# Pinning TensorE's order by unit, moving mask and output steps behind maxima, and one subtraction to GpSimd, in an attention and token-mixing kernel

## Chip, cores and metric

One core of a Trainium2 chip. The metric is the device time of one launch in microseconds (us). The engines are TensorE (PE in the profile; its weight loads are PEld), VectorE (DVE), ScalarE (ACT), GpSimd (POOL) and SyncE (SP), which issues DMAs.

## What is computed

Three stages, cut to what matters (B = 2, H = 8, S = 768, D = 64, 16 clusters, model width 512, all float32):

```python
def _attn_ref(q, k, v, centroids):
    q_n, k_n, c_n = (x / (norm(x) + 1e-6) for x in (q, k, centroids))
    q_assign = argmax(einsum('bhsd,hcd->bhsc', q_n, c_n), -1)
    k_assign = argmax(einsum('bhsd,hcd->bhsc', k_n, c_n), -1)
    mask = q_assign[:, :, :, None] == k_assign[:, :, None, :]
    scores = where(mask, scale * q @ k.transpose(0, 1, 3, 2), -1e9)
    attn = exp(scores - max(scores, -1))
    return attn / (sum(attn, -1) + 1e-9) @ v

def _moe_ref(x, w_tok1, w_tok2, w_ch1, w_ch2):
    u = x + (relu(x.transpose(0, 2, 1) @ w_tok1) @ w_tok2).transpose(0, 2, 1)
    return u + relu(u @ w_ch1) @ w_ch2

def _moe2_ref(x, w_theta, w_tok_r, w_tok_i, w_ch):
    theta = x @ w_theta
    u = x + w_tok_r @ (x * cos(theta)) + w_tok_i @ (x * sin(theta))
    return u + relu(u @ w_ch)
```

A query attends only to the keys of its own cluster. The attention's output is the x of the second stage, whose output is the x of the third.

## The kernel before

Attention runs over 48 units of 256 queries of one head (`units`, three per head, six per pair of heads). A loop over n issues three stages of three neighbouring units. `scores(n)` (L385) makes two tiles s in PSUM, each of 128 queries by 768 keys: each half of 384 keys is a product of the query with the key and its low part (L392 and L397; qh, k1) and a second one that carries the query's low part and the one-hot rows of the clusters (L398; q2, k2), with a large negative number where clusters differ. VectorE takes the maximum of a tile (nm, L400), ScalarE the exponential (e, L402). `turn(n-1)` (L411) transposes e of the unit before in 12 products into three tiles t of the pool ps_t (L417), which ScalarE (two) and VectorE (one) copy to p (L420, L422). `values(n-2)` (L426) multiplies p with v into o (L438), 12 products; its two halves are added by tmp on ScalarE (L445) and an addition on VectorE into xt (L447). PSUM holds two banks of s (ps_s), three of t (ps_t, which sim, pp and x use too) and one of o (ps_o).

Around these three stand other steps. `masks` (L238) is a generator, of which the loop takes two steps for each n: similarities of q and k with the centroids (sim, L246), their transposing on VectorE (sT, L252), maximum (mx, L256), equality (eq, L259) and transposing (eqT, L265), a product with a triangular matrix (pp, L270) that keeps the first maximum of equal ones, the one-hot rows (oh, L271) and m (L286); `place` copies the rows of m by DMA into q2 and k2 (L358). `natural` (L453) transposes xt of a finished pair of heads back into rows (x, six products in two banks of ps_t, L460) and VectorE multiplies them with the reciprocal sums into xn (L462). `split_pair` and `prep` load and split the next q and k (GpSimd, DMAs of SP). `load_w` (L100) loads and repairs weights: L109 and L110 on ScalarE, L112 and L113 on VectorE, L116, L80 and L86 on GpSimd or VectorE. For the first head the one-hot rows are written by engines and not by DMA (L276 and L280 on ScalarE, L279 on VectorE), and `prep_pair_first` (L309) splits the key by L314 and L316.

After attention come the token products (`tok_up` g, with gh on ScalarE at L147 and gl on VectorE at L148; `tok_down` h; `tok_x` splits x by xh, L84, and xl, L86), then the channel products and the third stage, all as triples of products of high and low parts (L126 to L128).

The order inside each engine is fixed when the program is built: a scheduler places the instructions by its own simulation, and `tc.issue_after(...)` ties a step behind a marked one. Each engine then runs its row in order, and waits at an instruction's head for what it needs.

## Time and profile before

| | |
|---|---|
| median of 3 runs | 665.26 us (663.36 to 665.73) |
| profiled execution | 664.99 us, span 663.3 us |
| TensorE busy | 646.8 us (98% of the span), 3591 products |
| TensorE weight loads | 517.7 us (78%) |
| VectorE busy | 401.2 us (60%) |
| ScalarE busy | 344.9 us (52%) |
| GpSimd busy | 257.6 us (39%) |

A row of the timeline gives the start in us, the duration, engine, line, operation, out<-in, tile size and how many stand in the row; in brackets the idle time of the engine before it and what released it. Ends of products on TensorE are modelled, so distances of starts are firmer than durations. The attention takes the first 240 us or so.

### The profile page before, as it was taken

To read this page: it belongs to the slowest core of one execution; us is meant where nothing else is said; L and a number is where in the kernel's file an instruction comes from. 1 tells how busy PE (TensorE), PEld (TensorE's weight loads), DVE (VectorE), ACT (ScalarE), POOL (GpSimd) and SP (SyncE) were. 2 spreads that over 40 slices of the span, in tenths; PEclk is the share of its full clock that TensorE was granted. 3 is DMA by queue.
4 is the path that set the end of the run, shared out by engine and by line. 5 is a ranking of instruction groups with operands and counts; after the bars stand their busy time and mean duration, and the time that the engine had idled before them with its cause. 6 is when DMAs were issued, how large, how long until landed. Compare 5 with 4: busy or idle time off the path is not lost.

```text
span 663.3 us, 9795 instructions
## 1 busy us (share of the span) xinstructions
PE 646.8 (98%) x3591; PEld 517.7 (78%) x3591; DVE 401.2 (60%) x649; ACT 344.9 (52%) x653; POOL 257.6 (39%) x231
## 2 busy tenths in 40 slices
PE   7999999999999989999999999999999999999998
PEld 4777777777777758878888888888887878888886
DVE  5877778687787776466665442546677694531212
ACT  5676776777767863256444320428487673320000
POOL 6230312364031131138887520603467796541000
PEclk9999999999999998999999999999999999999999
DMA  8554755444555121023433310310021424300001
GB/s 294 160 138 105 169 123 144 120 117 114 113 123 124 37 96 47 18 67 124 154 133 127 126 53 14 95 33 0 1 85 42 128 88 127 114 20 33 16 33 47
DMA packets 24207, 61.42 MB, mean 93 GB/s; under 512 B 4256, under 2 KB 7520, under 8 KB 24160
## 3 DMA queue, kind: packets, MB, share of 16 engines
q1 hardware_dynamic: 24160, 60.80, 32.3%
q8 instruction: 28, 0.46, 0.3%
q14 instruction: 19, 0.16, 0.1%
HBM read 39.65 MB, written 3.15 MB: 65 GB/s over the span
## 4 chain that ended last, share of the span: by engine, by line
PE 86%; ACT 4%; DVE 3%; POOL 3%; issue 2%; DMA 2%; SPq 0%; POOLq 0%; ACTq 0%
PE o L438 10%; PE t L417 9%; PE s L397 5%; PE r L126 5%; PE r L127 5%; PE r L128 5%; PE c L126 5%; PE c L127 5%; PE c L128 5%; PE s L398 5%; PE y L128 4%; PE y L127 4%; PE y L126 4%; PE po L126 2%; PE po L128 2%
## 5 line engine op out<-in xcount | busy, mean ns | idle before, releaser
L402 ACT ACTIVATE e<-s,nm 128x768 f32<-128x768 f32 x96 | 86.7, 905 | 29.4 <-DVE nm L400 28.1
L400 DVE TENSOR_REDUCE nm<-s 128x1 f32<-128x768 f32 x96 | 90.5, 951 | 18.9 <-PE s L398 18.0
L417 PE MATMUL t<-ident,e 128*128 128x128 f32 x576 | 80.5, 275 | 0.6 <-ACT p L420 0.5
L417 PEld LDWEIGHTS t<-ident,e 128*128 128x128 f32 x576 | 66.4, 140 | 16.0 <-issue 9.4
L397 PE MATMUL s<-k,qh 128*128 128x384 f32 x188 | 71.9, 382 | 2.5 <-ACT e L402 2.3
L438 PE MATMUL o<-p,vs 128*64 128x256 f32 x564 | 71.2, 388 | 0.0
L398 PE MATMUL s<-k,q 128*128 128x384 f32 x192 | 65.3, 343 | 2.4 <-DVE q L279 2.4
L420 ACT ACTIVATE p<-t 128x512 f32<-128x512 f32 x96 | 52.2, 594 | 25.4 <-PE t L417 25.0
L126 PE MATMUL r<-ul,c_h 128*128 128x512 f32 x144 | 56.5, 396 | 0.4 <-DVE ul L90 0.4
L126 PE MATMUL y<-zl,k_h 128*128 128x512 f32 x144 | 56.1, 390 | 0.0
L128 PE MATMUL y<-zh,k_h 128*128 128x512 f32 x144 | 56.1, 390 | 0.0
L127 PE MATMUL r<-uh,c_l 128*128 128x512 f32 x144 | 56.1, 390 | 0.0
L127 PE MATMUL y<-zh,k_l 128*128 128x512 f32 x144 | 56.0, 389 | 0.0
L127 PE MATMUL c<-c_h,rl 128*128 128x512 f32 x144 | 56.0, 390 | 0.0
L128 PE MATMUL r<-uh,c_h 128*128 128x512 f32 x144 | 56.0, 390 | 0.0
L128 PE MATMUL c<-c_h,rh 128*128 128x512 f32 x144 | 55.9, 390 | 0.0
L126 PE MATMUL c<-c_l,rh 128*128 128x512 f32 x144 | 55.2, 391 | 0.0
L438 PEld LDWEIGHTS o<-p,vs 128*64 128x64 f32 x564 | 36.3, 136 | 22.7 <-issue 5.9
L116 POOL TENSOR_TENSOR c_f<-c_f,c_raw 128x512 uint32<-128x512 uint32 x24 | 31.6, 1318 | 44.7 <-issue 31.3
L80 POOL TENSOR_SCALAR qh<-ql 128x768 fp32r<-128x768 f32 x7 | 5.8, 835 | 100.9 <-DMA qh<-qh 100.8
L397 PEld LDWEIGHTS s<-k,qh 128*128 128x128 f32 x188 | 35.4, 188 | 11.1 <-ACT e L402 5.6
L398 PEld LDWEIGHTS s<-k,q 128*128 128x128 f32 x192 | 36.7, 192 | 3.8 <-ACT k L276 3.4
(192 smaller groups left out, 1387.9 us busy)
## 6 DMA issues: line engine op xcount, KB each, us to landing
c_raw<-wc SPq DMA_DIRECT2D x24, 512.0 KB, 3.3
k_raw<-wri SPq DMA_DIRECT2D x18, 512.0 KB, 3.5
qh<-qh SPq DMA_DIRECT2D x28, 192.0 KB, 3.0
k<-kh SPq DMA_DIRECT2D x28, 192.0 KB, 3.8
ql<-qT SPq DMA_DIRECT2D x8, 384.0 KB, 3.2
kl<-kT SPq DMA_DIRECT2D x8, 384.0 KB, 4.6
vs<-v SPq DMA_DIRECT2D x16, 192.0 KB, 2.4
w_raw<-w SPq DMA_DIRECT2D x6, 512.0 KB, 4.1
```

Of the source, the lines that this page charges most:

```text
L80: nc.gpsimd.tensor_scalar(out=h, in0=x, scalar1=1.0, scalar2=0.0, op0=ALU.mult, op1=ALU.add)
L116: nc.gpsimd.tensor_tensor(out=wu, in0=wu, in1=lo, op=ALU.add)
L126: nc.tensor.matmul(ps, ah, bl, start=first and i == 0, stop=False)
L127: nc.tensor.matmul(ps, al, bh, start=False, stop=False)
L128: nc.tensor.matmul(ps, ah, bh, start=False, stop=last and i == n - 1)
L397: nc.tensor.matmul(ps[:, half, :NH], qh[:, c], k1[:, n], start=True, stop=False)
L398: marks["scores"] = nc.tensor.matmul(ps[:, half, :NH], ql[:, c], kk[:, n], start=False, stop=True)
L400: marks["max"] = nc.vector.tensor_reduce(out=nm, in_=ps[:, :, :NH], axis=AX.XY, op=ALU.max, negate=True)
L402: marks["exp"] = nc.scalar.activation(out=e.rearrange("p (a n) -> p a n", a=2), in_=ps[:, :, :NH], func=AF.Exp, bias=nm, accum_out=sums[b, ...
L417: marks["turn"] = nc.tensor.transpose(ps[:, a, i * P : i * P + P], es[i][:, kt * P : kt * P + P], ident)
L420: marks["pA"] = nc.scalar.activation(out=p, in_=ps, func=AF.Copy)
L438: nc.tensor.matmul(po[r : r + 64, :], vs[:, kt, :], pr[kt // 2][:, kt % 2, :], start=kt < 2, stop=kt >= NT - 2, tile_position=(0, r),)
```

## The change

It has four parts.

1. In `prep_pair_first` the subtraction that makes the first key's low part (64 x 768) is issued by GpSimd and no longer by VectorE; the mark "k1", behind which `clear(1)` is issued, is now that subtraction.
2. For the first unit's scores, all products and not only the second ones are issued behind the first one-hot product (pp).
3. `scores(n)` is issued behind the last product of `values` issued before it, and `turn(n-1)` behind the last product of `scores(n)` (for n > 2).
4. `natural` of a pair comes two steps of the loop later (n + 3 for n + 1) and behind the last maximum issued before; the masks' two steps of a loop step move from ahead of `turn` to the end of the loop step, behind a maximum as well.

```diff
@@ prep_pair_first
-            marks["k1"] = nc.gpsimd.tensor_scalar(out=k1[0:64, :], in0=k, **one)
+            nc.gpsimd.tensor_scalar(out=k1[0:64, :], in0=k, **one)
             nc.scalar.activation(out=qh[0:64, :], in_=q, func=AF.Copy, scale=scale)
-            nc.vector.tensor_tensor(out=k1[64:128, :], in0=k, in1=k1[0:64, :].bitcast(F32), op=ALU.subtract)
+            marks["k1"] = nc.gpsimd.tensor_tensor(out=k1[64:128, :], in0=k, in1=k1[0:64, :].bitcast(F32), op=ALU.subtract)
@@ scores
-                if first:
-
-                    for half in range(2):
-                        nc.tensor.matmul(ps[:, half, :NH], qh[:, c], k1[:, half * NH : half * NH + NH], start=True, stop=False)
                 with tc.issue_after(marks["cl"].ins) if first else nullcontext():
                     for half in range(2):
                         n = slice(half * NH, half * NH + NH)
-                        if not first:
-                            nc.tensor.matmul(ps[:, half, :NH], qh[:, c], k1[:, n], start=True, stop=False)
+                        nc.tensor.matmul(ps[:, half, :NH], qh[:, c], k1[:, n], start=True, stop=False)
@@ values
-                    nc.tensor.matmul(
+                    marks["o"] = nc.tensor.matmul(
@@ the loop over n
                 if n != 1:
-                    es[n] = scores(b, h, u, ops[b, h])
+                    with tc.issue_after(marks["o"].ins) if "o" in marks else nullcontext():
+                        es[n] = scores(b, h, u, ops[b, h])
...
-            if n >= 3:
-                for _ in range(PACE):
-                    next(gen, None)
...
-                prs[n - 1] = turn(*units[n - 1], es.pop(n - 1))
+                with tc.issue_after(marks["scores"].ins) if n > 2 else nullcontext():
+                    prs[n - 1] = turn(*units[n - 1], es.pop(n - 1))
...
-                    late.append((n + 1, b, h // 2))
+                    late.append((n + 3, b, h // 2))
             while late and (n >= late[0][0] or n == len(units) + SKEW - 1):
                 _, b, pr = late.pop(0)
-                natural(b, pr)
+                with tc.issue_after(marks["max"].ins):
+                    natural(b, pr)
+            if n >= 3:
+
+                with tc.issue_after(marks["max"].ins):
+                    for _ in range(PACE):
+                        next(gen, None)
```

Three places show what the scheduler makes of it. Lines of the changed kernel are lower by five from the scores on (L392 and L393 for L397 and L398, L412 for L417, L433 for L438, L440 for L445, L455 for L460).

First, TensorE at the start, behind the first similarities. Before:

```order
L392 MATMUL s_194<-k_169,qh_168 128x384 x2
L392 MATMUL s_203<-k_169,qh_168 128x384 x2
L270 LDWEIGHTS ltri
L270 MATMUL pp_183<-eqT_180,ltri 128x384
L398 MATMUL s_194<-k_0_151,q_0_149 128x384
L398 MATMUL s_203<-k_0_151,q_0_149 128x384
```

Changed:

```order
L270 LDWEIGHTS ltri
L270 MATMUL pp_183<-eqT_180,ltri 128x384
L392 MATMUL s_194<-k_169,qh_168 128x384
L392 MATMUL s_203<-k_169,qh_168 128x384
L393 MATMUL s_194<-k_0_151,q_0_149 128x384
L392 MATMUL s_194<-k_169,qh_168 128x384
L393 MATMUL s_203<-k_0_151,q_0_149 128x384
L392 MATMUL s_203<-k_169,qh_168 128x384
```

The one-hot product (pp) stands ahead of all products of the two first tiles, and the second halves of the products with qh stand among those with the one-hot rows.

Second, TensorE in a unit in the middle of attention (o: values, s: scores, t: transposes). Before:

```order
L438 MATMUL o_537<-p_472,vs_249 64x256 x2
L438 MATMUL o_537<-p_479,vs_249 64x256 x2
L438 MATMUL o_537<-p_486,vs_249 64x256 x2
L397 MATMUL s_549<-k_454,qh_453 128x384
L398 MATMUL s_549<-k_0_151,q_0_149 128x384
L397 MATMUL s_549<-k_454,qh_453 128x384
L398 MATMUL s_549<-k_0_151,q_0_149 128x384
L417 MATMUL t_594<-ident,e_505 128x128 x2
L417 MATMUL t_601<-ident,e_505 128x128 x2
L417 MATMUL t_608<-ident,e_505 128x128 x2
L397 MATMUL s_558<-k_454,qh_453 128x384
L398 MATMUL s_558<-k_0_151,q_0_149 128x384
```

Changed:

```order
L433 MATMUL o_537<-p_472,vs_249 64x256 x2
L433 MATMUL o_537<-p_479,vs_249 64x256 x2
L433 MATMUL o_537<-p_486,vs_249 64x256 x2
L392 MATMUL s_549<-k_454,qh_453 128x384
L393 MATMUL s_549<-k_0_151,q_0_149 128x384
L392 MATMUL s_549<-k_454,qh_453 128x384
L393 MATMUL s_549<-k_0_151,q_0_149 128x384
L392 MATMUL s_558<-k_454,qh_453 128x384
L393 MATMUL s_558<-k_0_151,q_0_149 128x384
L392 MATMUL s_558<-k_454,qh_453 128x384
L393 MATMUL s_558<-k_0_151,q_0_149 128x384
L412 MATMUL t_594<-ident,e_505 128x128 x2
```

The unit's eight score products stand together, and all transposes behind them. In the order of before, 21 output groups are followed by transposes and 18 by scores; now one and 32.

Third, ScalarE at the end of attention (gh: the token product's split; w_2, c_0: weights; xh: splits of x). Before:

```order
L445 ACTIVATE tmp_3247<-olast 64x256
L147 ACTIVATE gh_3286<-g_3267 128x512
L109 ACTIVATE w_2_f<-w_2_raw 128x512
L84 ACTIVATE xh_3312<-xn_72 128x512
L84 ACTIVATE xh_3316<-xn_73 128x512
L147 ACTIVATE gh_3308<-g_3267 128x512
L84 ACTIVATE xh_3320<-xn_74 128x512
```

Changed:

```order
L440 ACTIVATE tmp_3247<-olast 64x256
L109 ACTIVATE w_2_f<-w_2_raw 128x512
L147 ACTIVATE gh_3286<-g_3267 128x512
L84 ACTIVATE xh_3312<-xn_72 128x512
L84 ACTIVATE xh_3316<-xn_73 128x512
L84 ACTIVATE xh_3320<-xn_74 128x512
L84 ACTIVATE xh_3324<-xn_75 128x512
L84 ACTIVATE xh_3328<-xn_76 128x512
L84 ACTIVATE xh_3332<-xn_77 128x512
L109 ACTIVATE c_0_f<-c_0_raw 128x512
L110 ACTIVATE c_0_raw<-c_0_raw 128x512
L147 ACTIVATE gh_3308<-g_3267 128x512
```

The second gh stands behind four more xh and behind two steps of the load of c_0. From the last transposes of attention on, TensorE's own order is the same in both.

## Rows read from the trace of the kernel before

**Rows 1.** Busy time by stretch: us, PE, PEld, DVE, ACT, POOL, PEclk, DMA share, GB/s

```profile
20.00:242.00 222.00, 218.99 (x1619) 167.04 (x1619) 171.15 (x300) 162.27 (x343) 57.41 (x50) 1.00 0.49 118
```

**Rows 2.** Timeline of TensorE, units in the steady stretch

```profile
62.90 1.52 PE L438 MATMUL o<-p,vs 128*64 128x256 f32 x12
...
67.20 1.51 PE L438 MATMUL o<-p,vs 128*64 128x256 f32 x12
...
83.12 0.47 PE L397 MATMUL s<-k,qh 128*128 128x384 f32 x1
...
84.65 1.47 PE L417 MATMUL t<-ident,e 128*128 128x128 f32 x12
86.05 1.52 PE L438 MATMUL o<-p,vs 128*64 128x256 f32 x12
87.50 0.66 PE L417 MATMUL t<-ident,e 128*128 128x128 f32 x4
```

**Rows 3.** List of TensorE's waits: total us, times, longest

```profile
PE s L397 <- ACT e L402: 2.3, 4, 0.6
```

**Rows 4.** Timeline of TensorE, one such wait

```profile
55.40 0.34 PE L398 MATMUL s<-k,q 128*128 128x384 f32 x1
56.36 0.44 PE L397 MATMUL s<-k,qh 128*128 128x384 f32 x1 [0.62 <-ACT e L402]
56.64 0.34 PE L398 MATMUL s<-k,q 128*128 128x384 f32 x1
```

**Rows 5.** Timeline of all engines, the start

```profile
6.90 0.49 PE L246 MATMUL sim<-kl,cst 128*32 128x384 f32 x2
7.65 0.95 DVE L316 TENSOR_TENSOR k<-kl,k 64x768 fp32r<-64x768 f32 x1 [0.72 <-POOL k L314]
9.84 0.56 DVE L259 TENSOR_TENSOR eq<-sT,mx 128x384 bf16<-128x384 f32 x1
11.63 1.80 POOL L306 TENSOR_TENSOR k<-kr,k 64x768 fp32r<-64x768 f32 x1
12.02 1.63 DVE L279 CAST q<-oh 16x384 fp32r<-16x384 f32 x1
12.07 1.06 ACT L276 ACTIVATE k<-oh 16x384 fp32r<-16x384 f32 x2 [1.36 <-DVE oh L271]
13.79 1.62 PE L398 MATMUL s<-k,q 128*128 128x384 f32 x4 [2.41 <-DVE q L279]
16.12 0.90 ACT L402 ACTIVATE e<-s,nm 128x768 f32<-128x768 f32 x1 [0.42 <-DVE nm L400]
```

**Rows 6.** Timeline of VectorE, the end of a pair

```profile
55.47 1.26 DVE L462 TENSOR_TENSOR xn<-x,ri 128x128 f32<-128x128 f32 x6
```

**Rows 7.** The page's costliest groups, then the timeline round a weight load

```profile
L400 DVE TENSOR_REDUCE nm<-s 128x1 f32<-128x768 f32 x96 | 90.5, 951 | 18.9 <-PE s L398 18.0
...
207.59 0.67 ACT L109 ACTIVATE w_f<-w_raw 128x512 f32<-128x512 f32 x1
208.15 0.70 ACT L110 ACTIVATE w_raw<-w_raw 128x512 uint32<-128x512 uint32 x1
210.33 0.42 DVE L447 TENSOR_TENSOR xt<-o,tmp 64x256 f32<-64x256 f32 x1
211.15 1.52 PE L438 MATMUL o<-p,vs 128*64 128x256 f32 x12
```

**Rows 8.** Timeline after attention

```profile
250.34 0.63 ACT L84 ACTIVATE xh<-xn 128x512 fp32r<-128x512 f32 x1 [0.65 <-PE g L126]
254.53 0.60 ACT L147 ACTIVATE gh<-g 128x512 fp32r<-128x512 f32 x1 [3.57 <-PE g L128]
255.03 2.19 ACT L84 ACTIVATE xh<-xn 128x512 fp32r<-128x512 f32 x4
255.16 0.69 DVE L148 SCALAR_TENSOR_TENSOR gl<-g,gh 128x512 fp32r<-128x512 f32 x1 [1.46 <-ACT gh L147]
256.38 0.39 PE L126 MATMUL h<-gl,w_h 128*128 128x512 f32 x1
```

## Prediction

> **What bounds the kernel now.** I read the busy time by stretch first. Between 20 and 242 us, the steady part of attention, TensorE is busy for 218.99 of 222.00 us, while VectorE, ScalarE and GpSimd are busy for 171.15, 162.27 and 57.41 us, at a granted clock of 1.00 [rows 1]. So the end is set by TensorE's row of instructions, and a change of order can do two things only: alter what a step costs TensorE (a switch from one kind of product to another), or take away and bring in waits. All that TensorE idles here is 3.0 us, 1.4% of the stretch.
>
> The timeline of TensorE gives the price of a unit [rows 2]. From one output group to the next, with transposes and scores interleaved, it is 67.20 - 62.90 = 4.30 us. Ungrouped pieces stand there too: eight scores 84.65 - 83.12 = 1.53, twelve transposes 86.05 - 84.65 = 1.40, an output group 87.50 - 86.05 = 1.45.
>
> The list of waits says what TensorE stood for: 2.3 us, four times, before scores for an exponential [rows 3]. The timeline shows one of them [rows 4]: the next unit's first score comes at 56.36 instead of right behind 55.40, since its bank holds scores whose exponential is late. Starts show more than the profile's idle does, because ends are modelled. The score products of a row follow each other by 0.17 (eight in 1.53, the first with a switch); here the distance is 56.36 - 55.40 = 0.96, and the one after it 56.64 - 56.36 = 0.28. So 0.79 + 0.11 = 0.90 is lost where 0.62 is counted: 1.45 for each us counted.
>
> **The change, part by part**, against the profiled execution (664.99 us, span 663.3), which is 0.27 below the median of 665.26.
>
> *Start.* The subtraction of the first key's low part (L316, 0.95 us) goes from VectorE to GpSimd. Behind it on VectorE stand the transposing of the similarities, their maximum and eq. TensorE's sim products end at 6.90 + 0.49 = 7.39 [rows 5], so these steps could run 1.2 us earlier, and eq at 8.64 instead of 9.84. But GpSimd's own subtraction of 64x768 takes 1.80 us (L306, of the same shape) and would run from 7.65 to 9.45, across eq. What such company costs is seen with the copy of the one-hot rows: 16x384 elements take 1.63 us, from 12.02 to 13.65, ending 0.22 after L306 does at 13.43 [rows 5]. So I let eq end at 9.9 instead of 10.40: 0.5 gained, and eqT, the product pp and oh behind it come 0.5 sooner. Before, TensorE's second products stood until 13.79, for the copy of 1.63 us; that copy now runs ahead of L306 instead of beside it, and the last to come are ScalarE's rows of the key, which ended at 12.07 + 1.06 = 13.13 and now end at 12.6. So this wait ends 1.1 sooner. But the second halves of the first products now stand behind pp and among the second products: two more are done before the first maximum can start. At the 1.62 / 4 = 0.4 that these take, 0.8 of the 1.1 is lost; at the 0.17 of a later score 0.3 is. The first exponential (16.12) so starts 0.3 to 0.8 sooner; I take the value nearer to the later one, **-0.7**. If eq is not held at all, 0.7 more is gained (-1.4); if the copy falls beside two GpSimd operations in a row, the start loses up to 0.5.
> The Trainium skill, "SBUF — State Buffer", section "SBUF: two separate sides", says that VectorE and GpSimd hold a shared port pair as an exclusive lock for a whole instruction, also for a VectorE operation with two SBUF inputs against one of GpSimd that reads SBUF. By that, eq would start only at 9.45 and end at 10.0, and the start would gain 0.6 instead of 0.7. The copy of 1.63 us beside GpSimd bears the rule out.
>
> *Order in a unit.* Scores now follow the last output product, and transposes follow the scores. By [rows 2] the grouped unit costs 1.53 + 1.40 + 1.45 = 4.38, against 4.30. In the order of before 20 units went from outputs to transposes and now go to scores; the others had the new sequence already. 20 x 0.08 = 1.6; the 1.53 has a product of the masks beside it, so I take **+1.5**, between 0 and 1.6. Grouping gains nothing: no piece is shorter in it.
>
> *Old waits.* The natural steps stood on VectorE ahead of a maximum (six multiplies, 1.26 us, from 55.47 [rows 6], just before the exponential was late); they now stand behind it. So do the masks' steps: each moves by a maximum (0.95 [rows 7]) at most, with the copies of m's rows that SP issues after them; those keep their place in SP's order and have several units until their head comes, so I cost the move at nothing. If they were late, their head's scores would wait up to 1 us for each pair. All of the 3.0 us goes, by starts 3.0 x 1.45: **-4.3** (-3.0 by the profile's idle).
>
> *New waits.* (a) The six multiplies of a pair now stand behind a maximum. The first group of x transposes (four) fills one of three banks of ps_t, the second (two) another, with scores of the next unit between; then that unit's transposes want the bank back. VectorE's chain is four multiplies (4 x 0.21), an addition of the output (L447, 0.42), a maximum (0.95 on average) and two multiplies (0.42) [rows 6, 7], 2.6 in all and 2.8 with the steps from engine to engine; TensorE has eight scores (1.53), two transposes of x (2 x 0.117) and two banks of unit transposes (8 x 0.117) [rows 2] in the same time, 2.7. That is 0.1 late, and 0.2 with the bank's own step; I take 0.2 for each of six pairs: +1.2; none if the maximum comes first, 1.15 if a second one comes between. (b) The single output bank is freed by tmp on ScalarE and the addition on VectorE. In two units weight loads (L109 0.67, L110 0.70) now stand ahead of tmp. The slack is seen at 210.33: the addition ends at 210.75 and the next outputs start at 211.15, 0.40 later [rows 7]. 1.37 - 0.40 = 0.97, of which I take 0.9 twice: +1.8. (c) The last pair's unit transposes wait behind four multiplies: +0.8. Together **+3.8**, between 0 and 9.5 (six times 0.95 more).
>
> *After attention.* The order of ScalarE puts the second gh behind four more xh and two steps of the load of c_0. In the profile of before, gh starts when TensorE's last g product is done (254.53), four xh take 2.19 from 255.03, gl ends at 255.85 and h, which reads it, starts at 256.38: 0.53 of slack [rows 8]. The xh wait for TensorE to finish with buffers (250.34, 0.65 idle), so not all of them can run ahead. At least c_0's two steps (0.67 + 0.70) delay gh: 1.37 - 0.53 = **+0.8**; at most all six, 2.19 + 1.37 - 0.53 = 3.0; nothing if buffers come free in time.
>
> Sum: -0.7 + 1.5 - 4.3 + 3.8 + 0.8 = +1.1, so 666.1 for the profiled execution and, 0.27 higher, **666.4 us** as a median. From the last transposes on TensorE's order is the same to the end, so nothing is added there.
>
> **Rivals.** 0.5% is 3.3 us, about what a measurement of this kernel can tell from no change.
>
> *A, the old waits go and nothing takes their place.* For it: VectorE has 51 us free in the stretch [rows 1], and 2.8 against 2.7 in (a) is close to even. Against: three banks and one output bank as before, and a weight load ahead of tmp. -0.7 + 1.5 - 4.3 = -3.5, so 661.5, as a median 661.8 us; without the 1.5 of order 660.3. It decides where VectorE gets x's second group multiplied before the unit's maximum. Chance 0.16.
>
> *B, slower: natural waits a whole maximum more.* The multiplies may begin only when a maximum is done, and maxima come in twos. If x's second group stands behind both, each pair costs 0.95 more: 6 x 0.95 = 5.7, so 671.8, as a median 672.1 us. It decides when VectorE is late by more than 0.5 us, half a maximum, at the pair's end. For it: the pairs' ends are where before was late, too [rows 4]. Against: the first unit behind a pair has 0.95 x 2 + 0.85 of work for VectorE in 4.3 us. Chance 0.10; 0.02 more for the ends of several bounds at once.
>
> *C, TensorE has room that the busy time hides.* Weight loads are busy only 167.04 of 222.00 us [rows 1]. If grouping let products run at the pace of their loads, up to 55 us would go: 610 us. Against: the grouped pieces cost 4.38 where interleaved ones cost 4.30 [rows 2]. Chance 0.01.
> The Trainium skill, "Perfetto Trace Analysis", section "Identifying the Most-Contended Engine", holds that matmul busy time is no good measure of what is left on TensorE, and that the busy share of weight loads is; here that would be 75%, and the pieces' rows do not bear out that order could win it.
>
> *Nothing moves* (the pinned order repeats what the scheduler had) is a case of the forecast: 665.3 us.
>
> **How the numbers follow.** The forecast, between 662 and 668.5, has 0.71. The lower end has to reach A, 661.0; the upper end takes in half of what B adds (2.9) and stops at 669.3; B and the rest beyond leave under 0.2 out. Faster: A and C, 0.17. Slower: 0.12.
>
> **What would show it.** In the new profile: the first exponential at 15.4, within 0.5, and GpSimd's subtraction at 7.65, 1.8 long. The waits of scores for exponentials, 2.3 us before, gone from the list. The unit of one output group to the next at 4.36 to 4.38. In their place short waits, on x or t for VectorE's multiplies at the pairs' ends, on o at two units with a weight load, and about 0.8 us at the first h. The busy time of TensorE in the stretch should stay within 2 us of 219. The prediction is wrong if the waits of TensorE in attention sum to under 1.5 or over 8 us, or if the grouped unit is under 4.25.

## The result, and the profile after

The changed kernel took 670.74 us (670.67 to 670.79, 3 runs) against 665.26: a ratio of 1.0084, interval 1.0063 to 1.0105. The forecast was no change, at 666.4 in a range up to 669.3; the changed kernel came out slower, and above that range. Run again in six more executions beside 20 of the kernel before, it took 667.19 against 663.81, 1.0052 [1.0033, 1.0071]: it is slower, by some 3.4 us. The profiled one of the first three executions held a further loss that will be found below; the other two left no trace, so that they had the same loss is likely by their times, but not shown.

The profiled execution of the changed kernel took 670.74 us, span 669.0. Lines from the scores on are lower by five than before (L392 and L393 scores, L412 t, L433 o, L457 xn; L643 and L644 make rh and rl in both). Page, busy time and instructions by engine:

```profile
PE 648.8 (97%) x3591; PEld 520.5 (78%) x3591; DVE 403.3 (60%) x648; ACT 341.7 (51%) x653; POOL 260.2 (39%) x232
```

TensorE does the same 3591 products in 648.8 us of work, 2 us more than before; the rest of the 5.7 us of span is idle. Busy time of the steady stretch, to lay beside [rows 1] (same columns):

```profile
20.00:242.00 222.00, 218.47 (x1615) 168.34 (x1609) 169.46 (x297) 158.05 (x339) 57.57 (x50) 1.00 0.48 118
```

The stretch looks the same: 3.5 us idle instead of 3.0. So most of the time was not lost in attention. The list of TensorE's waits over the whole execution (us in total, times, longest) says where idle time went:

```profile
PE g L126 <- DVE gl L148: 3.8, 1, 3.8
PE o L433 <- DVE xt L442: 2.1, 3, 1.2
...
PE c L126 <- ACT rh L643: 1.3, 1, 1.3
...
PE t L412 <- DVE xn L457: 1.0, 4, 0.5
...
PE c L127 <- DVE rl L644: 0.8, 1, 0.8
PE h L126 <- DVE gl L148: 0.6, 1, 0.6
```

The waits of scores for exponentials [rows 3] are gone; one of 0.3 stands at the start, ahead of that stretch. Waits of o on the output addition and of t on x's multiplies stand in their place, as foreseen. Three groups stand after attention: g on gl (2.6 us before), h on gl, which the prediction had, and c on rh and rl, which no part of it had. None of the signs that the prediction named for being wrong came: from 20 to 242 us the waits of TensorE come to 3.1 us, and an ordinary unit takes 4.34 to 4.42. What broke the forecast lies behind attention.

A better way to place the loss than busy time is to lay the starts of the same products beside each other. Where the distance grows, time is lost:

| start of | before | changed | difference |
|---|---|---|---|
| first output product | 24.05 | 22.71 | -1.34 |
| last output product | 242.62 | 242.35 | -0.27 |
| first u (transposes after the token products) | 270.66 | 272.57 | +1.92 |
| c, 145th product (channel products, second round) | 382.91 | 384.82 | +1.92 |
| c, 169th product | 388.52 | 394.51 | +5.99 |
| last po product (end) | 659.82 | 665.56 | +5.74 |

So -1.34 at the start, +1.07 in attention, +2.19 in the 28 us after it, +4.07 within 24 channel products at 385 us, -0.25 behind. The loss of 4.07 us lies 140 us behind the last product of attention.

That loss in the timelines of TensorE and ScalarE of the changed kernel (start, us, engine, line, operation, idle before and releaser):

```profile
386.64 0.39 PE L128 MATMUL c<-c_h,rh 128*128 128x512 f32 x1
388.32 0.47 PE L126 MATMUL c<-c_l,rh 128*128 128x512 f32 x1 [1.29 <-ACT rh L643]
389.60 0.50 PE L127 MATMUL c<-c_h,rl 128*128 128x512 f32 x1 [0.81 <-DVE rl L644]
...
390.80 0.63 PE L128 MATMUL c<-c_h,rh 128*128 128x512 f32 x1
```

```profile
382.42 0.60 ACT L643 ACTIVATE rh<-r 128x512 fp32r<-128x512 f32 x1
386.49 0.65 ACT L110 ACTIVATE th_raw<-th_raw 128x512 uint32<-128x512 uint32 x1 [3.47 <-DMA th_raw<-wth]
387.04 0.64 ACT L109 ACTIVATE th_f<-th_raw 128x512 f32<-128x512 f32 x1
387.59 1.07 ACT L643 ACTIVATE rh<-r 128x512 fp32r<-128x512 f32 x2
```

ScalarE stands 3.47 us for a load of w_theta that nobody needs yet; rh, which TensorE needs, is next but one in its row. TensorE waits 1.29 and 0.81 us, then works at half clock for a while (products of 0.63 for 0.39; the granted clock is 0.53 from 392 to 394, so nearly all of that at the lower of its two levels, 1.2 for 2.4 GHz). In the kernel before, the same load was ready at 382.10 and rh just in time. The load came late because the stream of weights, in which each load waits for a buffer of the third one ahead, had lost 2.1 us at one load of 512 KB. The DMA view of that load's stretch (queue, packets, MB, share; then the issue, KB and us from issue to landing), changed kernel, from 352.0 to 357.2:

```profile
q1 hardware_dynamic: 205, 0.71, 38.9%
q8 instruction: 1, 0.02, 1.1%
...
c_raw<-wc SPq DMA_DIRECT2D x1, 512.0 KB, 5.2
```

and of the same load in the kernel before, from 349.5 to 354.7:

```profile
q1 hardware_dynamic: 212, 0.74, 40.7%
...
c_raw<-wc SPq DMA_DIRECT2D x1, 512.0 KB, 3.1
```

In the first there is one packet of instructions, 16 KB that some 256 of TensorE's instructions take, and the load needs 5.2 us for 3.1. In the packets of the trace it runs from 354.44 to 355.32; eight packets of the load then run one behind the other from 355.30 to 357.1, when all its others were done at 355.3. The trace names no DMA engine for a packet: that these eight stand behind the instructions on one of the 16 is read from their times. In the kernel before the nearest such packet came at 355.37, 2.7 us behind the load's last.

So I had two theories. **F**: the loss at 386 us is a late load (by a meeting with a packet of instructions) that reaches TensorE because rh stands behind a step waiting for loads on ScalarE; what is left is the order of gl after attention. **R**: the loss is rival B's, multiplies behind maxima, and whatever is seen later follows from it.

### The profile page after: what moved, and what is told of

The parts are those of the page before. It is cut to its first block, busy times and chain, and to the rows that moved or that the text cites. A ratio compares the mean times of both kernels' runs of the same rounds, so it can differ in the third digit from the quotient of the medians.

```text
span 669.0 us, 9862 instructions
## 1 busy us (share of the span) xinstructions
PE 648.8 (97%) x3591; PEld 520.5 (78%) x3591; DVE 403.3 (60%) x648; ACT 341.7 (51%) x653; POOL 260.2 (39%) x232
## 5 line engine op out<-in xcount | busy, mean ns | idle before, releaser
L397 ACT ACTIVATE e<-s,nm 128x768 f32<-128x768 f32 x96 | 86.8, 904 | 21.7 <-DVE nm L395 21.5
L415 ACT ACTIVATE p<-t 128x512 f32<-128x512 f32 x96 | 54.9, 596 | 37.9 <-PE t L412 37.2
L412 PE MATMUL t<-ident,e 128*128 128x128 f32 x576 | 72.4, 273 | 1.4 <-DVE xn L457 1.0
L433 PE MATMUL o<-p,vs 128*64 128x256 f32 x564 | 71.2, 388 | 2.1 <-DVE xt L442 2.1
L392 PE MATMUL s<-k,qh 128*128 128x384 f32 x192 | 71.5, 373 | 0.4 <-ACT e L397 0.3
L412 PEld LDWEIGHTS t<-ident,e 128*128 128x128 f32 x576 | 65.7, 141 | 5.4 <-PE t L412 2.8
L393 PE MATMUL s<-k,q 128*128 128x384 f32 x192 | 65.3, 341 | 0.9 <-ACT k L276 0.9
L433 PEld LDWEIGHTS o<-p,vs 128*64 128x64 f32 x564 | 36.3, 136 | 23.9 <-issue 5.0
L392 PEld LDWEIGHTS s<-k,qh 128*128 128x128 f32 x192 | 36.3, 189 | 18.8 <-issue 7.6
L651 DVE TENSOR_TENSOR xn<-c,xn 128x512 f32<-128x512 f32 x36 | 24.5, 687 | 26.2 <-PE c L128 26.1
L393 PEld LDWEIGHTS s<-k,q 128*128 128x128 f32 x192 | 36.7, 191 | 1.2 <-ACT k L276 1.2
```

What stands on the lines that cost most here:

```text
L392: nc.tensor.matmul(ps[:, half, :NH], qh[:, c], k1[:, n], start=True, stop=False)
L393: marks["scores"] = nc.tensor.matmul(ps[:, half, :NH], ql[:, c], kk[:, n], start=False, stop=True)
L397: marks["exp"] = nc.scalar.activation(out=e.rearrange("p (a n) -> p a n", a=2), in_=ps[:, :, :NH], func=AF.Exp, bias=nm, accum_out=sums[b, ...
L412: marks["turn"] = nc.tensor.transpose(ps[:, a, i * P : i * P + P], es[i][:, kt * P : kt * P + P], ident)
L415: marks["pA"] = nc.scalar.activation(out=p, in_=ps, func=AF.Copy)
L433: marks["o"] = nc.tensor.matmul(po[r : r + 64, :], vs[:, kt, :], pr[kt // 2][:, kt % 2, :], start=kt < 2, stop=kt >= NT - 2, tile_position ...
```

## The experiments

What each run gave, by its median and its ratio to the kernel before as run beside it (medians of the kernel before: 663.93 beside e1 to e4, 663.81 beside f1 to g1, 663.93 beside h1 to h4, 663.58 beside i1 to i3), and by its profile: start of the first output product; from there to the last one; from there to the first u; and from the 145th to the 169th c product.

| run | us | ratio, interval | first o | to last o | to first u | c stage |
|---|---|---|---|---|---|---|
| before | 665.26 | | 24.05 | 218.57 | 28.04 | 5.61 |
| changed | 670.74 | 1.0084 [1.0063, 1.0105] | 22.71 | 219.64 | 30.22 | 9.69 |
| f1 changed again | 667.19 | 1.0052 [1.0033, 1.0071] | 23.16 | 219.65 | 30.27 | 6.22 |
| e1 fewer warm | 667.52 | 1.0053 [1.0035, 1.0072] | 24.65 | 219.53 | 30.32 | 6.03 |
| f3 more warm | 668.57 | 1.0074 [1.0054, 1.0095] | 22.61 | 219.63 | 30.24 | 6.42 |
| e2 before, more warm | 663.60 | 0.9997 [0.9978, 1.0016] | 23.49 | 218.51 | 28.02 | 6.08 |
| e3 gl first | 664.90 | 1.0019 [0.9995, 1.0042] | 22.98 | 219.56 | 26.75 | 6.34 |
| e4 start alone | 663.46 | 0.9991 [0.9971, 1.0010] | 24.15 | 218.52 | 28.05 | 5.88 |
| f2 rh first | 665.63 | 1.0034 [1.0020, 1.0048] | 23.02 | 219.59 | 30.28 | 5.44 |
| g1 gl and rh first | 663.85 | 0.9998 [0.9984, 1.0013] | 22.65 | 219.59 | 29.51 | 5.44 |
| h1 before, rh first | 663.31 | 0.9986 [0.9970, 1.0002] | 25.39 | 218.51 | 26.46 | 5.44 |
| h2 no part four | 669.27 | 1.0071 [1.0052, 1.0090] | 24.23 | 223.61 | 27.47 | 6.40 |
| h3 no part three | 658.55 | 0.9913 [0.9890, 0.9937] | 23.06 | 213.81 | 28.02 | 6.03 |
| h4 waits repaired | 659.29 | 0.9922 [0.9903, 0.9940] | 22.75 | 216.04 | 26.01 | 5.44 |
| i1 turn tied only | 665.75 | 1.0025 [1.0011, 1.0040] | 23.05 | 219.45 | 29.06 | 7.25 |
| i2 scores tied only | 668.48 | 1.0069 [1.0053, 1.0086] | 23.06 | 221.73 | 29.80 | 6.13 |
| i3 no part three, rh first | 656.44 | 0.9890 [0.9872, 0.9909] | 22.76 | 213.86 | 26.41 | 5.44 |

### e1 and f3: moving the packets of instructions

```diff
-WARM = (17, 4, 20, 9)
+WARM = (13, 4, 16, 5)      # e1
+WARM = (17, 4, 26, 18)     # f3
```

> The changed kernel with 12 dummy products fewer at the start (17 to 13, 20 to 16, 9 to 5, all in front of the first exponential), nothing else. Theory F (a transfer of TensorE's instructions, 16 KB on one DMA engine at 354.4 us, falls on the load of the weights c_raw, the load ends 2 us late, and TensorE loses 4.1 us at 386 to 394 us): with 24 instructions fewer ahead, the same transfer comes some 2.7 us later in the program, behind the load; the wait of the down products for rh and rl (1.3 + 0.8 us) and the half clock behind it go, and the time falls by about 4, to 666.7 (665.5 to 667.5). Theory R (the loss is that of rival B, multiplies and masks behind maxima in attention, and what is lost later follows from being late): nothing changes but the start, 670.7 within 1 us, and the wait at 386 stays.

> The changed kernel with 15 dummy products more at the start (20 to 26 and 9 to 18). In the kernel before that brought the first outputs 0.57 us sooner, and in the changed kernel 12 fewer brought them 1.94 us later. Theory F: the instruction transfer moves 3.4 us ahead of where it was, off or onto the load by an amount that the executions decide; the first outputs between 22.2 and 22.7 us; 666.0 to 670.5. Theory R: 670.2 to 670.7.

e1: 667.52, the c stage down from 9.69 to 6.03, no wait of over 0.2 us at it; the load that took 5.2 us takes 3.1. The loss at 386 went, while attention stayed (219.53): for F. But its first output came 1.94 us later, 1.5 of them at half clock behind the first exponential (0.50 granted from 18 to 20 us), so the total alone would have said little; that the missing dummy products brought the half clock about is not shown. f3 also had 6.42, and 0.10 us gained at the first output; another wait, th on x2h in the third stage, took 2.6 us. f1, though, the changed kernel itself, has a c stage of 6.22 in another execution: the meeting is no property of the kernel but of an execution, so neither e1 nor f3 proves that the shift of 24 or 30 instructions did it.

### e2: the same in the kernel before

```diff
-WARM = (17, 4, 20, 9)
+WARM = (17, 4, 26, 18)
```

> The kernel before with 15 dummy products more at the start (20 to 26 and 9 to 18), nothing else. Theory F: its transfer of instructions at 355.4 us, which came 2.7 us behind the load, comes some 3.4 us earlier in the program and falls on the load, if it is not thrown past it: a wait of some 2 us for rh and rl appears round 385 us and the time rises by 3 to 4, to 668.5 to 670 with up to 1 us of the start in it. Theory R: no more than the start's own cost, up to 1 us: 665.3 to 666.3.

A miss for F: 663.60, no late load (3.5 us), a c stage of 6.08. The packet came at 352.1, 3.1 us behind the issue, on the load's last part, and cost it 0.4. The time of such a packet moves by a few us against the program by itself, so it can't be aimed. The 0.57 us that the first output gained is not told from nothing in the total.

### e4: the start alone

The first two hunks of the change (prep_pair_first and scores), and neither of the others:

```diff
-            nc.vector.tensor_tensor(out=k1[64:128, :], in0=k, ...)
+            marks["k1"] = nc.gpsimd.tensor_tensor(out=k1[64:128, :], in0=k, ...)
```

> The kernel before with the first two parts alone: the first key's low part by GpSimd, the one-hot product ahead of all scores. Theory F: the first output group comes 1.3 us sooner than before (22.7 for 24.05), TensorE keeps that through attention, and the end is 1.3 us sooner, 664.0 (profiled span 662), unless a transfer of instructions meets a load of weights now. Theory R: the same at the start; no difference at 386.

Parts one and two alone bring the first exponential to 14.93 for 16.12, and the first transposes to 16.81 for 17.97; but the first output comes at 24.15 for 24.05. Half clock takes the gain back (0.50 granted from 18 to 20 us). It is no matter of the parts that are missing: from the first transposes to the first output TensorE's order is the same as in the changed kernel, and h3 below has the same wait of 1.8 us for the exponential ahead of them, but a clock of 1.00, and its first output comes at 23.06. h1, whose start is that of the kernel before, has half clock there too, and 25.39 for 24.05. So the column of first outputs holds up to 1.5 us of clock, and the gain is read better at the first exponential.

### e3: gh and gl ahead, after attention

```diff
-                    for i in range(NT // 2):
+                    for i in range(NT // 2 - 1):
                         w2s.append(load_w(...))
...
             tok_up(0, t, ...)
+            if t == 0:
+                with tc.issue_after(marks["gh"].ins), tc.issue_after(marks["gl"].ins):
+                    w2s.append(load_w(w2[:, :, 512:768], "w2_2", "pv"))
         for s in range(NT):
-            tok_x(1, s, part, "av")
+            with tc.issue_after(marks["gh"].ins) if s > 1 else nullcontext():
+                tok_x(1, s, part, "av")
```

> The changed kernel, with the third load of w_tok2 behind the first gl, and the splits of x 2 to 5 (and with them the load of c_0) behind the second gh, as in the kernel before. Theory F: the waits at the first g (3.83 us) and at h (0.62 us) fall to about 2.6 and 0, so the first u comes 2 us sooner than in the changed kernel (270.6 for 272.57). The transfer of instructions and the load of c_raw both move with it, so the 4 us at 386 may stay: 668.6, or 664.6 if they pass each other. Theory R: the waits after attention are not the cause and TensorE gets it back nowhere: 670.7 within 1 us.

The wait at g fell to 2.86 and that at h went; the first u came at 269.29, 3.3 us sooner than in the changed kernel, 1.3 more than expected. In the changed kernel these rows show what was late (ScalarE, VectorE, TensorE; beside [rows 8]):

```profile
246.14 0.67 ACT L109 ACTIVATE w_f<-w_raw 128x512 f32<-128x512 f32 x1 [2.98 <-DVE w_l L86]
246.84 0.60 ACT L147 ACTIVATE gh<-g 128x512 fp32r<-128x512 f32 x1
...
248.19 0.68 DVE L113 SCALAR_TENSOR_TENSOR w_f<-w_f,w_raw 128x512 uint32<-128x512 uint32 x1
248.79 0.69 DVE L148 SCALAR_TENSOR_TENSOR gl<-g,gh 128x512 fp32r<-128x512 f32 x1
...
249.53 0.50 PE L126 MATMUL g<-xl,w_h 128*128 128x512 f32 x1 [3.83 <-DVE gl L148]
...
256.72 0.59 ACT L147 ACTIVATE gh<-g 128x512 fp32r<-128x512 f32 x1
258.16 0.50 PE L126 MATMUL h<-gl,w_h 128*128 128x512 f32 x1 [0.62 <-DVE gl L148]
```

The first gh (245.77 before) stands behind L109 of w_tok2's third load, which waits for a buffer, and gl (247.79 before) behind L113 of the same load: 1.0 us later, though attention ended 0.27 sooner, so that the wait of g grew from 2.57 to 3.83. The second gh is 2.2 us later than [rows 8], behind xh and c_0. The rest of e3's gain is the clock. The same 4 us behind the wait at g, by the busy-time view (columns as [rows 1]), in the changed kernel and in e3:

```profile
249.50:253.50 4.00, 3.97 (x11) 3.20 (x12) 2.35 (x4) 2.00 (x4) 1.42 (x2) 0.63 0.44 131
```

```profile
248.70:252.70 4.00, 3.95 (x17) 3.30 (x18) 1.78 (x4) 1.27 (x2) 1.93 (x2) 1.00 0.11 23
```

11 products in one, 17 in the other. The clock did not fall in e3 after a wait of 2.86 us, but did in the kernel before after 2.57 (0.57 granted from 248.5 to 252.5) and in g1 at one of 2.86. What decides it is left open. To the first u it is worth 1.6 us between the kernel before and h1 (28.04 and 26.46), and 2.8 between g1 and e3 (29.51 and 26.75), pairs with the same order there.

### f1: the changed kernel again

No edit.

> The changed kernel itself once more, in more executions, beside the kernel before: e1 to e4 showed executions of one kernel to spread by 4 to 6 us. Theory F: the instruction transfer meets the load of c_raw in some executions and not in others, so the times spread from about 666.5 to 671, and the wait for rh and rl at 386 is there or not with them; median 669. Theory R: the times stand close to 670.7, with the waits of attention unchanged.

667.19 (665.96 to 668.31): a spread as F says, but lower than the 669 it gave, and none of these six reached 670.7. The waits of attention and after it are the same to 0.3 us; the c stage is 6.22 instead of 9.69.

### f2: rh ahead of the loads of w_theta

```diff
+    rows = marks["rh"], marks["rl"]
...
-            wt = [load_w(wth[:, c * 512 : c * 512 + 512], f"th_{c}") for c in range(NC)]
+            with tc.issue_after(rows[0].ins), tc.issue_after(rows[1].ins):
+                wt = [load_w(wth[:, c * 512 : c * 512 + 512], f"th_{c}") for c in range(NC)]
```

> The changed kernel with the four loads of w_theta ordered behind the last rh and rl of the second round of channel products, so that no rh stands behind a ScalarE step that waits for a load; TensorE's order is the same. Theory F: a late load no longer reaches TensorE at 386, whatever the instruction transfer does: the 1.3 + 0.8 us of waits for rh and rl and the half clock behind them go, 666.7 and a smaller spread. Theory R: 670.7, as the changed kernel.

665.63, 1.6 us under f1, with a c stage of 5.44 us and no wait in it; the c stage makes 0.8 of the difference in these two profiles. All five kernels with this edit (f2, g1, h1, h4, i3) have 5.44 us there, all without it 5.61 to 9.69.

### g1: both repairs

e3's and f2's edits together.

> The changed kernel with both repairs: the first and second gh and gl ahead of other work (as in e3), and the loads of w_theta behind rh (as in f2). Theory F: e3's gain of 3.3 us after attention and no loss at 386: first u at 269.3, span 661.0 to 661.8, time 663.0, under the changed kernel by 5 or more and 0.9 under the median of the kernel before in the runs beside e1 to e4 (663.93). Theory R: 667.5, since the loss at 386 would not hang on the loads.

663.85, as the kernel before beside it (663.81), 0.9 above the expectation; in the profiled execution half clock at g took some 2.8 us of e3's gain back. By chance this run gives the cleanest test of F: its load was late too. From 350.9 to 356.3:

```profile
q8 instruction: 1, 0.02, 1.1%
...
c_raw<-wc SPq DMA_DIRECT2D x1, 512.0 KB, 5.0
```

and with rh ahead of the loads ScalarE did not make TensorE wait for it (timeline of ScalarE):

```profile
384.57 0.58 ACT L647 ACTIVATE rh<-r 128x512 fp32r<-128x512 f32 x1
385.04 0.67 ACT L109 ACTIVATE th_f<-th_raw 128x512 f32<-128x512 f32 x1
385.60 1.78 ACT L110 ACTIVATE th_raw<-th_raw 128x512 uint32<-128x512 uint32 x3
```

A late load of 5.0 us, and a c stage of 5.44. So the late load costs nothing by itself, and 4 us where rh stands behind it. Theory R falls with this: attention was the same in g1, 219.59.

### h1: f2's edit in the kernel before

> The kernel before with f2's edit alone (the loads of w_theta ordered behind the last rh and rl of the second round of channel products). Theory G (the changed kernel's +3.4 us is 1.8 from the order of gh and gl after attention and 1.6 from rh behind the loads of w_theta, with attention itself even): the waits for rh and rl are a matter of being late, so the kernel before gains less than the changed one did, 0 to 1 us: 662.8 to 663.8. Rival H (rh behind the loads costs every kernel the same in the mean, and the changed kernel's excess has another place): 1.6 us gained here as well, 662.2.

663.31 against 663.93: 0.6 us in the median, as G has it, but the interval (0.9970 to 1.0002) takes in H's 1.6 as well as nothing. Whether the kernel before gains less by it than the changed one is left open.

### h2 and h3: part four without three, and three without four

```diff
# h2: natural and masks as before
-                    late.append((n + 3, b, h // 2))
+                    late.append((n + 1, b, h // 2))
...
# h3: no ties of TensorE's order
-                    with tc.issue_after(marks["o"].ins) if "o" in marks else nullcontext():
-                        es[n] = scores(b, h, u, ops[b, h])
+                    es[n] = scores(b, h, u, ops[b, h])
...
-                with tc.issue_after(marks["scores"].ins) if n > 2 else nullcontext():
-                    prs[n - 1] = turn(*units[n - 1], es.pop(n - 1))
+                prs[n - 1] = turn(*units[n - 1], es.pop(n - 1))
```

> The changed kernel without its fourth part: outputs' transposes and multiplies one step behind their pair and masks' steps ahead of turn, as before. From the first output product to the last one TensorE took 218.57 us in the kernel before and 219.5 to 219.65 in every run with the changed order. Theory G: the waits on x's multiplies (0.31 us at six pairs) go, and the waits of scores for exponentials that follow a late maximum (0.9 us at three pairs) come back: 219.5 to 220.5. Rival H: part four is pure loss in attention, so its removal gives 217.7.

> The changed kernel without its third part (TensorE's order not pinned by unit), the rest as changed. Theory G: interleaved units are 0.05 to 0.08 us cheaper, at some 20 units, so the stretch from the first output product to the last is 1 to 1.5 us shorter, 218.1 to 218.6, unless a new wait takes it back. Rival H: without the pinning waits return in attention, 220 or more.

Both expectations were far off, and these runs tell most. From the first output product to the last, with parts one and two in all four: neither part 218.52 (e4), part three alone 223.61 (h2), part four alone 213.81 (h3), both 219.64. So part four saves 4.7 us and, behind part three, 4.0; part three costs 5.1 and, beside part four, 5.8. Without part three the change is 5.4 us faster than the kernel before: 0.9913. TensorE's waits in attention from 20 us on, in h2 and then in h3:

```profile
PE t L412 <- DVE xn L457: 4.6, 7, 0.7
PE t L412 <- ACT p L415: 1.0, 2, 0.7
PE x L455 <- ACT p L415: 0.9, 1, 0.9
PE o L433 <- DVE xt L442: 0.7, 1, 0.7
```

```profile
PE t L412 <- DVE xn L457: 0.3, 1, 0.3
```

h3 waits once, for 0.3 us. Equal stretches in the middle tell the rest. Two pairs of heads (12 units) take 56.15 us before, 56.23 changed, 57.24 in h2 and 54.93 in h3 (h3 from 115.34 to 170.28). What is different in the changed kernel at a pair's end (timelines of TensorE and VectorE):

```profile
60.34 0.66 PE L455 MATMUL x<-ident,xt 128*128 128x128 f32 x4
...
61.54 0.38 PE L455 MATMUL x<-ident,xt 128*128 128x128 f32 x2
...
62.46 1.80 PE L412 MATMUL t<-ident,e 128*128 128x128 f32 x12
64.19 1.51 PE L433 MATMUL o<-p,vs 128*64 128x256 f32 x12
```

```profile
61.03 0.89 DVE L457 TENSOR_TENSOR xn<-x,ri 128x128 f32<-128x128 f32 x4 [0.80 <-PE x L455]
61.83 0.40 DVE L442 TENSOR_TENSOR xt<-o,tmp 64x256 f32<-64x256 f32 x1
62.16 0.94 DVE L395 TENSOR_REDUCE nm<-s 128x1 f32<-128x768 f32 x1
63.03 0.47 DVE L457 TENSOR_TENSOR xn<-x,ri 128x128 f32<-128x128 f32 x2
```

The last two multiplies, on which a bank of ps_t hangs, start at 63.03, behind the addition and the maximum; twelve transposes in a row want three banks at 62.46 and take 1.73 us for 1.40, that is 0.33 to 0.35 of wait at each of six pairs, by starts. In h3 all six products of x stand together and scores between the unit's transposes, so the multiplies start sooner and a late bank is asked for later (timeline of TensorE, h3):

```profile
115.34 1.52 PE L433 MATMUL o<-p,vs 128*64 128x256 f32 x12
116.79 0.87 PE L455 MATMUL x<-ident,xt 128*128 128x128 f32 x6
...
120.31 1.52 PE L433 MATMUL o<-p,vs 128*64 128x256 f32 x12
```

This unit takes 4.97 us in h3 and 5.30 in the changed kernel (58.89 to 64.19). The rest of the difference lies in one more unit of each pair, the one with the eight similarities (sim): 5.35 in the changed kernel, where sim stands between the unit's two tiles of scores (72.89 to 78.24, sim from 75.24), and 5.09 in h3, where it stands right behind the outputs (128.95 to 134.04, sim from 130.39). The four other units of a pair take 17.45 us in the changed kernel and 17.41 in h3: grouping or interleaving an ordinary unit makes no difference that counts. So beside part four, part three costs by where x and sim come to stand and, towards the end of attention, by waits that h3 has not (o on the output addition, 1.24 and 0.75 us by starts, and the last transposes, 1.0).

### i1 and i2: the halves of part three

i1 has the first of h3's two edits (scores not tied behind outputs), i2 the second (transposes not tied behind scores):

```diff
# i1
-                    with tc.issue_after(marks["o"].ins) if "o" in marks else nullcontext():
# i2
-                with tc.issue_after(marks["scores"].ins) if n > 2 else nullcontext():
```

> The changed kernel without the first half of part three (scores not tied behind outputs; transposes still tied behind the unit's scores). From the first to the last output product TensorE took 219.64 us in the changed kernel and 213.81 without the whole of part three (h3). Theory P (the tie of the transposes costs it: with all 12 behind both tiles of scores, the three banks of ps_t are asked for in one row, so x's multiplies, p's copies and output additions are late for it): 219 to 220 here, time 667. Rival Q (the tie of scores behind outputs costs it): 213.5 to 214.5, time 658.5 to 660.

> The changed kernel without the second half of part three (transposes not tied behind the scores; scores still tied behind outputs). Theory P: transposes go between the two tiles of scores again, 213.5 to 214.5 us from the first to the last output product, and the time is 658.5 to 660. Rival Q: 219 to 220 and 667.

Neither P nor Q holds: either tie alone keeps the cost. Two pairs take 56.23 us with the first tie undone and 56.77 with the second, where both undone give 54.93. In i2 the waits of t on x's multiplies are even longer (some 0.45 at each of six pairs, by starts). A new wait comes at the end of attention, too: x on the output addition, 3.7 us in i1 and 4.5 in i2, which makes their middle columns hard to compare.

### h4 and i3: versions that beat both

h4 is g1 with x's second group one step later and the loads of w_tok1 behind the last tmp and addition:

```diff
-                    late.append((n + 3, b, h // 2))
+                    late.append((n + 3, b, h // 2, ((0, 4),)))
+                    late.append((n + 4, b, h // 2, ((4, 2),)))
...
-                with tc.issue_after(marks["exp"].ins):
+                with tc.issue_after(marks["tmp"].ins), tc.issue_after(marks["xt"].ins):
                     i = len(w1s)
```

> g1 (both repairs), and two more: x's second group (two transposes, two multiplies) one loop step behind the first, and the loads of w_tok1 behind the last tmp and output addition. Theory G: the waits on x's multiplies (0.31 us at six pairs) and those of outputs behind the weight loads (1.23 and 0.75) go, 3.5 us in all, so the stretch from first to last output product is 216 to 216.5 and the time 660.3 (659.5 to 661.5), under both kernels. Rival H: a freed wait comes back as another one; 219 to 219.6 for the stretch and 663.9.

659.29, a little under the range expected: the waits on x and o go, 219.59 becomes 216.04, with part three still in place.

i3 is h3 with f2's edit.

> h3 (parts one, two and four) with f2's edit (rh ahead of the loads of w_theta). Theory F with G: 0.6 us less than h3 as it was in h1 against the kernel before, up to 1.6 as in f2 against the changed kernel: 657 to 658, the fastest of all. Rival: nothing on top of h3, 658.6, since TensorE in h3 lost only 0.4 us at this place.

656.44, the fastest: 0.9890 [0.9872, 0.9909], 7.1 us under the kernel before and 0.6 under the range expected.

## Why the prediction was wrong, point by point

*Start, -0.7 within -1.4 to +0.5.* The first exponential came at 14.78 for 16.12, -1.34, at the gainful end, in part by luck. The rows of VectorE and GpSimd, changed kernel:

```profile
6.65 2.39 POOL L316 TENSOR_TENSOR k<-kl,k 64x768 fp32r<-64x768 f32 x1
...
8.60 0.85 DVE L259 TENSOR_TENSOR eq<-sT,mx 128x384 bf16<-128x384 f32 x1
...
11.14 0.38 DVE L279 CAST q<-oh 16x384 fp32r<-16x384 f32 x1
```

eq was held as forecast: GpSimd's subtraction ran 2.39 us, to 9.04, and eq ended 0.41 behind it instead of after its own 0.56. That is what the Trainium skill, "SBUF — State Buffer", section "SBUF: two separate sides", calls an exclusive lock, and the rows agree. GpSimd's operation began at 6.65 and not at 7.65, since in this execution the key came early enough for GpSimd's first step on it (L314, at 5.74) to start ahead of a VectorE step with two inputs (L318, at 5.83), which was held instead. In f1 L318 was first (5.97 and 6.05): there GpSimd's subtraction began at 7.70, took 1.81, eq again ended 0.41 behind it, at 9.92, and the first exponential came at 15.24, nearly the prediction's 7.65, 1.80, 9.9 and 15.4. So the mechanism was right, and 0.5 of the 1.34 belongs to this one execution. The copy of the one-hot rows, ahead of L306, took 0.38 for 1.63.

*Order +1.5, old waits -4.3, new waits +3.8: +1.0 in attention.* Measured +1.07 (218.57 to 219.64). By starts the new waits are 0.34 at six pairs (2.0; the prediction had 1.2), 1.24 and 0.75 of o behind weight loads (2.0; it had 1.8), and 1.0 at the end (0.8): 5.0 for 3.8. So order and old waits came to -3.9 together for the -2.8 forecast, and that the sum is right to 0.1 us is luck, since two errors of more than 1 us cancel. The term of order was too high: an ordinary grouped unit took 4.34 to 4.36 for the 4.38 that was added up, the interleaved ones before 4.30 to 4.36. The rows of (b), with ScalarE's two steps of the load ahead of tmp, and the addition that frees the output bank:

```profile
206.47 0.67 ACT L109 ACTIVATE w_f<-w_raw 128x512 f32<-128x512 f32 x1
207.02 0.71 ACT L110 ACTIVATE w_raw<-w_raw 128x512 uint32<-128x512 uint32 x1
207.75 0.38 ACT L440 ACTIVATE tmp<-o 64x256 f32<-64x256 f32 x1
...
209.97 0.42 DVE L442 TENSOR_TENSOR xt<-o,tmp 64x256 f32<-64x256 f32 x1
...
210.44 1.52 PE L433 MATMUL o<-p,vs 128*64 128x256 f32 x12 [1.16 <-DVE xt L442]
```

The division by parts was wrong as well: the prediction charged the waits on x's multiplies to part four. h3 shows that part four without the pinning has next to none of them, so they belong to part three.

*After attention, +0.8.* Measured +2.19: the wait of g on the first gl, 1.26 us longer behind a weight load, was not in the sum, though the order of ScalarE shown ahead had the load in front of gh; the second, with 0.62 of wait, was. This is a term mis-sized, within its own upper bound of 3.0.

*"From the last transposes on TensorE's order is the same to the end, so nothing is added there."* This is the step that failed. TensorE's order was the same, but what it waits for is set by the other engines: ScalarE's rh stood behind a load, by then the kernel was 1.9 us later, and in the profiled execution a load was 2.1 us late. The kernel before stood there with rh just in time. 4.07 of the 5.74 us came at this place in the profiled execution. In more executions it is less: f2 against f1 gives 1.6 us.

*Rival B*, slower at 672.1, had the sign and nearly the time, for another reason: the multiplies never waited for a second maximum (0.34 per pair and not 1.15). Rival A's 661.8 asked that no wait take the old ones' place; h3 is that, at 658.55, and needs the pinning away. Rival C is out: grouped units were not cheaper (4.34 to 4.36 us).

The loss in the median adds up: of f1's 3.4 us, 1.6 go with f2's edit and another 1.8 with e3's in g1, which is even with the kernel before. This is what the repairs give back; since the kernel before may gain by f2's edit too (h1: 0.6 us, not clear of noise), how much of the 1.6 the change itself brought is open.

## What to carry to other kernels

When an order is changed, look past the last instruction that moves: find the places downstream where an engine that the bound one waits for stands behind a step waiting for a load that is not needed yet, and put that step behind. Test the parts of a change that is meant as one against each other: here one part saved 4.0 to 4.7 us and another cost 5.1 to 5.8, and the sum looked like nothing. Lay the starts of equal instructions beside each other before reading lists of waits, since a table of where the distance grows finds a loss that lies 140 us behind the stage that was changed.

## What the runs showed of the hardware that I had not expected

- TensorE's own instructions come by DMA, 16 KB at a time, each for some 256 instructions (28 packets for 7182 products and weight loads), and by the times of the packets on an engine that carries the loads as well. The Trainium skill, "Runtime: NRT & Kernel Launch", section "Instruction fetch mechanics", tells of these blocks and calls the cost of crossing one mostly hidden; for TensorE's own supply the traces agree, in that no wait in its lists is for its own instructions, but a load of 512 KB that met one took 5.2 and 5.0 us instead of 3.1. It need not: f2's load of the same place, with a packet in its last 0.6 us, took 3.1. Over the 14 profiles of before, changed and e1 to h4, the loads of c_raw that met such a packet had a median of 3.78 us from issue to landing (31 loads), the others 3.22 (305); a part of that may be that a longer load is likelier to meet one.
- Executions of one kernel spread by 4.7 us here (661.82 to 666.53 for 51 executions of the kernel before), so that three executions can agree to 0.1 us and still lie 3.5 from the median of six others.
- At waits of 2.5 to 2.9 us at the first g the granted clock fell to half in some executions (0.50 to 0.60 over the next 4 us) and stayed at full in others (1.00), worth 1.6 to 2.8 us. Between the first exponential and the first output it did the same, worth 1.1 to 1.5 us (e1, e4, h1, h2).
